# One list replaced: a hand-over of the emission order of a fused SSM convolution and SwiGLU kernel

## The chip, the cores and the metric

The kernel runs on one core of a Trainium2 chip. The metric is the time of one execution on the device in microseconds (us). The engines are called as in the profile: PE (TensorE's matmuls) and PEld (its weight loads), DVE (VectorE), ACT (ScalarE), POOL (GpSimd) and SP (SyncE, which here only issues transfers).

## The reference

Everything is bf16 with S = 2048 rows, D = 640 columns and F = 1728 hidden columns. The first half is a gated long convolution, the second a SwiGLU layer, both with a residual:

```python
k_shift = sum(k_pad[:, t:t + S] * shift_k[:, 3 - t] for t in range(4))   # 4 taps down the rows
kv = k_shift * v
y = irfft(rfft(kv, 2 * S) * rfft(ssm_k, 2 * S))[:S]      # causal convolution, one filter of S taps a column
h = x + layernorm(x) * (y + kv * ssm_D)                  # x is A_q
n = layernorm(h)
out = h + (silu(n @ w_gate) * (n @ w_up)) @ w_down
```

## The kernel before

**Tiling.** The 2048 rows are cut into 4 blocks of 512. A block's columns of numbers are turned into a spectrum by matmuls with a constant basis WF (512 x 512, loaded once) and back by WI. `X0` to `X3` are the spectra of the blocks of kv, `G0` to `G3` those of the blocks of the filter ssm_k. Block j of the convolution needs X0 G_j + X1 G_(j-1) + ... + X_j G_0, which DVE multiplies and adds up (`mac`, L707 and L746/L747). Then come `inverse` (L813: matmuls with WI at L878, DVE's L892 that gates with the normalised row and adds the residual, giving h), the second layernorm (`norm` L760 on POOL for a few small numbers a row, `applied` L802 on DVE or ACT for the rows, L804/L807), `turn_h` (L911: h is transposed, by PE at L926 or by a DMA at L919) and `ffn` (L966). The FFN of block j (called f0 to f3) runs beside the convolution of block j + 1; f3 alone has nothing beside it.

**FFN.** The 1728 hidden columns are 13 chunks of 128 and one of 64. Two chunks at a time are computed for gate and up (`by_four` L1001; matmuls at L1022): ACT takes the silu of the gate's PSUM tile (L1014) and copies the up tile (L1012), DVE multiplies (L1016). Chunk 12 and the last 64 columns are done by `odd_by_four` (L1025). In f3 its steps have these numbers: 880 and 881 are the projections of chunk 12's gate and up into the two halves of one PSUM tile, 882 the silu of the first half (L1032), 883 the copy of the second half (L1033), 884 their product; 885 to 888 are the same for the last 64 columns (L1037 to L1039). The down projection (L1110) goes row tile by row tile through three cuts of the 14 chunks (in f3, row tile 0: 889 to 891, and so on). For the last row tile of f3 each cut is made in two parts, the first 384 columns and the last 256: 904, 906 and 908 are the three cuts of the first part, 905, 907 and 909 of the second. DVE adds the residual out of PSUM (910 for the first part, 912 for the second, both L1127) and SP sends each part out (911, 913, L1129). In the other blocks ACT copies the sum (L1116) and POOL issues a DMA that adds it to the output (L1117).

**The plan and its order.** Every step above is one of 914 numbered steps of a plan (`Plan`), each a small group of instructions of one engine or one transfer. `ORDER` (L71 to L107) is a list of all 914 numbers. The kernel emits the steps in that sequence, so each engine executes its own steps in the sequence of the list, and a DMA queue starts its transfers so. A negative entry -n stands for step n - 1 done on its other engine:

```python
            if n < 0:
                op.eng, op.ns, op.fn = op.other
                if op.rest:
                    op.rest.fn = None
```

The other engine of an ACT eviction (a copy out of PSUM; `evict` L256, `taken` L354) is DVE. That of a weight load on SP (`load` L264, `load_w` L932) is POOL's DMA queue. That of one of ACT's two shifted copies of k per block (`load_two` L546, `put` L561) is a DMA that POOL issues (L563). That of an `applied` step on ACT is DVE. A product of k and v may read PSUM straight on DVE, in place of ACT's copy and DVE's multiply (L658 in place of L664 and L665).

The list also sets the buffers: there are 12 large SBUF buffers (`big`, used for inputs, spectra, weights and h), 5 row buffers (`row`) and 4 PSUM tiles of two banks (`ps`), and `Plan.schedule` (L189) gives each step that opens a buffer the one that has been free longest by the order of the list. Waits between engines follow from the buffers and data, not from the list's numbers.

**Queues.** SP issues the input loads, the constants, the transposing transfers of k and h, most weights and the last output rows, one behind the other; a load whose buffer is still in use holds up those behind it. POOL computes the norms' small numbers and the diagonal fills `pairs` (steps 17 to 21, L1185, each four tensors of 128 x 64) for the convolution of k by taps, and issues the adding DMAs and the weights and copies moved to it.

**Start.** The first loads are k0, g0, x0, v0 and WF (step 28), then by the list 366 (the last gate and up columns of f0), 205 (x1) and 30 (the negated basis, `minus`). PE turns k0 (L610), turns g0 (L471), does the taps of k0 (L639), and begins X0 at 13.21 us.

Of the kernel before, what the change touches and what calls it, by code (L numbers as in the profile page):

```python
# [68 lines left out]
TW = PAD + BLK  # L69
CUTS = ("X0", "G0", "m", "i")  # L70
ORDER = [  # L71
# [36 lines left out]
SLOTS = {'S': 8, 'big': 12, 'kT': 0, 'tT': 1, 'row': 5, 'sg': 0, 'co': 2, 'ps': 4, 'sm': 6}  # L108
HOME = {t: "big" for t in ("scr", "x", "ld", "t4", "hT", "wgu", "diag")} | {"o": "row", "ps_c": "ps", "ps_f": "ps"}
SPLIT = ((0,), (1,))  # L110
# [1220 lines left out]
```

## Time and profile before

Three executions of the kernel before gave a median of 262.64 us, 262.58 to 263.24. The profiled execution took 262.15 us.

| | |
|---|---|
| profiled execution: its own time | 262.15 us |
| its span, first to last instruction | 260.3 us |
| what lies around the span | 1.85 us |
| mean granted TensorE clock | 0.996 |
| PE busy | 251.7 us, 97% |
| DVE busy | 199.8 us, 77% |
| ACT busy | 180.3 us, 69% |
| POOL busy | 102.3 us, 39% |
| X0 begins (first L375) | 13.21 us |
| f0's projections begin (first L1022) | about 50.7 us |
| last matmul ends | 256.37 us |

Stages are read off PE's timeline: 0 to 13.2 is loading, k0 and g0; 13.2 to 50.7 the spectra X0, G0, G1 and X1, the taps of k1 and block 0 up to its transposed h; from there to 238 FFN projections and down projections lie between the matmuls of the later blocks' convolutions, and from 211 on f3 is alone; 238 to 256.4 is the last chunk and the down projection of f3, and the rest the last add and transfer. In the profile a PE group counts as busy from its first to its last matmul, so a wait of some tens of ns between matmuls shows as a lower pace and not as idle time. The idle time ahead of a group stands in brackets with what ended it.

### The profile page before, as it was taken

The numbers are of one execution on the slowest core, as the hardware profiler recorded it, in microseconds if no ns is written. First come the engines' busy times: TensorE is split into PE (matmuls) and PEld (weight loads), VectorE is DVE, ScalarE is ACT, GpSimd is POOL, SyncE is SP. The second block draws the span as 40 slices with busy tenths as digits, with TensorE's granted clock in tenths as the row PEclk, the third lists the DMA queues.
The fourth block names the chain that finished last, engine by engine and source line by source line (L and its number), as shares of the span: only waits on it lengthen the run. The fifth ranks groups of instructions, "written<-read, shape, count | busy, mean of one in ns | idle before, by whom it ended". The sixth has DMA issues, their size and how long they took to land.

```text
span 260.3 us, 4687 instructions
## 1 busy us (share of the span) xinstructions
PE 251.7 (97%) x1802; PEld 154.4 (59%) x1818; DVE 199.8 (77%) x262; ACT 180.3 (69%) x296; POOL 102.3 (39%) x114
## 2 busy tenths in 40 slices
PE   8999899999999999999999999999999999998993
PEld 7967567654655577754564577544457754443672
DVE  4589999999999999999999999999998100013113
ACT  3798999989999897797887987354595034446000
POOL 7952740007817983613029943129950041000000
PEclk9999999999999999999999999999999999999998
DMA  6996999979999999798958867769394575000002
GB/s 222 389 255 127 274 269 345 187 191 290 297 227 195 238 213 131 166 189 210 220 105 158 231 168 167 152 148 221 71 280 102 113 186 81 0 0 0 3 25 76
DMA packets 64335, 45.05 MB, mean 173 GB/s; under 512 B 30997, under 2 KB 59930, under 8 KB 64314
## 3 DMA queue, kind: packets, MB, share of 16 engines
q1 hardware_dynamic: 58576, 32.96, 51.0%
q0 software_dynamic: 5728, 11.80, 23.4%
q8 instruction: 14, 0.23, 0.4%
q14 instruction: 7, 0.06, 0.1%
q10 hardware_dynamic: 10, 0.01, 0.0%
HBM read 30.01 MB, written 4.59 MB: 133 GB/s over the span
## 4 chain that ended last, share of the span: by engine, by line
PE 84%; ACT 6%; DMA 4%; DVE 3%; issue 1%; SPq 1%; DVEq 0%; ACTq 0%
PE ps L1022 44%; PE ps L1110 23%; PE ps L375 10%; PE ps L878 4%; DMA WF<-const_wf 4%; PE ps L648 2%; ACT S L364 2%; ACT big L364 1%; DVE row L892 1%; ACT big L473 1%; DVE big L905 0%; ACT co L1012 0%; PE ps L471 0%; DVE big L658 0%; ACT big L928 0%
## 5 line engine op out<-in xcount | busy, mean ns | idle before, releaser
L1022 PE MATMUL ps<-big,big 128*128 128x512 bf16 x524 | 119.3, 379 | 1.8 <-ACT co L1033 1.0
L1022 PEld LDWEIGHTS <-big 128*128 128x128 bf16 x540 | 52.5, 98 | 61.3 <-issue 1.3
L1110 PE MATMUL ps<-wd,tT 128*128 128x320 bf16 (+2 forms) x416 | 60.6, 299 | 0.0
L1110 PEld LDWEIGHTS <-tT 128*128 128x128 bf16 x416 | 40.7, 98 | 16.3
L1016 DVE TENSOR_TENSOR tT<-tT,co 128x2048 bf16<-128x2048 bf16 x12 | 14.6, 1219 | 34.3 <-ACT tT L1014 28.7
L375 PE MATMUL ps<-big,WF 128*128 128x320 bf16 x240 | 39.1, 298 | 1.3 <-ACT big L364 1.0
L1014 ACT ACTIVATE tT<-ps 128x1024 bf16<-128x1024 f32 x24 | 24.4, 1025 | 19.8 <-PE ps L1022 19.7
L747 DVE TENSOR_TENSOR S<-S,big 128x2560 bf16<-128x2560 bf16 x23 | 34.3, 1492 | 0.8
L746 DVE TENSOR_TENSOR big<-S,S 128x2560 bf16<-128x2560 bf16 x23 | 34.1, 1484 | 0.2
L1012 ACT CAST co<-ps 128x1024 bf16<-128x1024 f32 x24 | 24.1, 1010 | 10.4 <-PE ps L1022 10.1
L375 PEld LDWEIGHTS <-WF 128*128 128x128 bf16 x240 | 23.1, 97 | 13.0 <-issue 2.0
L757 ACT ACTIVATE row<-big 128x640 bf16<-128x640 bf16 x32 | 23.7, 741 | 3.4 <-DVE big L905 1.4
L1117 POOL DMA_DIRECT2D out_dram<-row x12 | 12.2, 1211 | 26.9 <-ACT row L1116 26.9
L807 ACT ACTIVATE row<-big,sm 128x640 bf16<-128x640 bf16 x21 | 19.0, 927 | 1.6 <-POOL sm L789 1.2
L364 ACT CAST S<-ps 128x640 bf16<-128x640 f32 (+1 forms) x35 | 19.0, 590 | 1.5 <-PE ps L375 1.5
L364 ACT ACTIVATE big<-ps 128x640 bf16<-128x640 f32 (+1 forms) x23 | 15.3, 714 | 2.2 <-PE ps L375 2.2
L1116 ACT CAST row<-ps 128x640 bf16<-128x640 f32 x12 | 8.0, 697 | 11.9 <-PE ps L1110 11.2
L278 POOL DMA_DIRECT2D big<-row x8 | 7.0, 929 | 21.5 <-DVE row L892 21.1
L1185 POOL TENSOR_SCALAR pairs<-row,taps 128x64 bf16<-128x64 bf16 x20 | 13.9, 718 | 0.1
L775 POOL TENSOR_TENSOR sm<-sm 128x4 f32<-128x4 f32 x6 | 12.4, 2070 | 2.8 <-ACT row L796 2.6
L892 DVE SCALAR_TENSOR_TENSOR row<-row,ps 128x640 bf16<-128x640 bf16 x16 | 12.7, 814 | 0.8 <-PE ps L878 0.7
L278 POOL DMA_DIRECT2D S<-big x2 | 2.6, 1288 | 26.6 <-ACT co L1012 19.6
(110 smaller groups left out, 339.6 us busy)
## 6 DMA issues: line engine op xcount, KB each, us to landing
big<-in_B_w_gate_dram SPq DMA_DIRECT2D x17, 320.0 KB, 5.8
big<-in_B_w_up_dram SPq DMA_DIRECT2D x15, 320.0 KB, 5.1
big<-in_B_w_up_dram POOLq DMA_DIRECT2D x9, 320.0 KB, 6.6
big<-in_A_ssm_k_dram SPq DMA_DIRECT2D x4, 640.0 KB, 6.7
big<-in_A_q_dram SPq DMA_DIRECT2D x4, 640.0 KB, 7.2
big<-in_A_v_dram SPq DMA_DIRECT2D x4, 640.0 KB, 5.8
big<-in_B_w_gate_dram POOLq DMA_DIRECT2D x7, 320.0 KB, 5.1
wd<-in_B_w_down_dram SPq DMA_DIRECT2D x1, 2080.0 KB
```

Of the source, the lines that this page charges most:

```text
L364: (lambda: nc.scalar.activation(dst(), src(), ACT.Copy, scale=2.0)) if twice else (lambda: nc.scalar.copy(dst(), src())),
L375: nc.tensor.matmul(ap(ps)[:, h, 0:NH], w, ap(src)[:, r, h * NH:(h + 1) * NH], start=(first and i == 0), stop=(last and i == len(rs) - 1), ...
L746: nc.vector.tensor_mul(flat2(b), X.part(xs), H.part(hs))
L747: f(A.part(dst), A.part(dst), flat2(b))
L757: act(825, lambda r=r, junk=junk: nc.scalar.activation(ap(junk), ap(x)[:, r, :], ACT.Square, scale=D ** -0.5, accum_out=sm(s, 1)[:, r:r + ...
L807: nc.scalar.activation(ap(row), ap(x)[:, r, :], ACT.Identity, bias=sm(s, 5)[:, r:r + 1], scale=sm(s, 4)[:, r:r + 1])
L892: nc.vector.scalar_tensor_tensor(two(ap(t)), two(ap(t)), 1.0, half(ap(ps)), op0=ALU.mult, op1=ALU.mult, accum_out=sm(s, 0)[:, r:r + 1])
L1012: act(1010, lambda ps=ps: nc.scalar.copy(ap(co)[:, at:at + 2, :], ap(ps)), src, [(co, gi % 2)])
L1014: act(1010, lambda ps=ps: nc.scalar.activation(ap(tT)[:, c:c + 2, :], ap(ps), ACT.Silu), src, [done(range(c, c + 2), ROWS)])
L1016: dve(1220, lambda: nc.vector.tensor_mul(ap(tT)[:, c - 2:c + 2, :], ap(tT)[:, c - 2:c + 2, :], ap(co)), [co], [done(range(c - 2, c + 2), R ...
L1022: nc.tensor.matmul(ap(ps)[:, i, :], ap(w)[:, k, off:off + P], ap(hT)[:, k, :], start=(k == 0), stop=(k == KT - 1))
L1110: nc.tensor.matmul(ap(ps)[:, hf, to:to + n], t, ap(wd)[:, c, col + (hf - hs[0]) * NH:col + (hf - hs[0]) * NH + n], start=(c == order[0]), ...
```

## The change

Only the list `ORDER` is replaced. Its first and last lines before and after:

```diff
 ORDER = [
-    23, 4, 0, 1, 2, 5, 7, 6, 22, 31, 3, 39, 40, 8, 29, 13, 26, 27, 14, 15, 37, 38, 10, 24, 12, 9, 28, 11, 42, 33, 35, 41, 36, 57,
-    366, 55, -35, 43, 137, -57, 133, 205, 30, 192, -59, 134, 59, -61, 49, 50, 46, 132, -45, 51, 130, 52, -48, 136, 200, 45, -54,
...
-    846, 855, 865, 841, 857, 864, 866, 872, 873, 849, 858, 876, 885, 886, 874, 875, 824, 819, 881, 883, 887, 880, 894, 895, 882,
-    884, 899, 889, 904, 905, 888, 900, 896, 897, 901, 890, 891, 906, 908, 907, 909, 898, 892, 902, 893, 903, 910, 911, 912, 913]
+    0, 2, 31, 1, 4, 5, 7, 10, 6, 8, 16, 13, 12, 11, 22, 29, 26, 37, 27, 14, 3, 15, 23, 28, 42, -39, 9, 35, -37, 24, 39, 205, 40,
+    33, 41, 34, 55, 57, -57, -59, 137, 59, 134, 49, 30, -61, 132, 43, -45, 50, 51, 19, 63, 46, 366, 45, 52, 64, 68, 136, -48, 130,
...
+    872, 873, 829, 845, 846, 836, 837, 858, 874, 864, 885, 886, 865, 880, 881, 841, 866, 882, 883, 887, 875, 899, 900, 884, 888,
+    901, 902, 903, 894, 889, 904, 895, 906, 890, 896, 908, 910, 911, 891, 897, 905, 892, 898, 893, 907, 909, 912, 913, 824]
```

The steps and what each computes stay the same; PE does the same matmuls in another sequence from its fourth step on. The steps that change engine or queue:

| steps | before | after |
|---|---|---|
| evictions of k0: 34 | DVE | ACT |
| evictions of k0: 36, 38 | ACT | DVE |
| evictions of X0: 69, 75, 86, 88 | DVE | ACT |
| evictions of X0: 77, 96 | ACT | DVE |
| `applied` of block 2: 515, 519 | DVE | ACT |
| `applied` of block 2: 517 | ACT | DVE |
| `applied` of block 3: 736 | DVE | ACT |
| one product of k3 and v3: 656 | ACT's copy and DVE's multiply | DVE straight out of PSUM |
| shifted copy of k3: 614 | SP's queue | POOL's queue |
| shifted copy of k3: 615 | ACT, an instruction | POOL's queue, a DMA |
| weights of f1: 525, 541, 549, 559, 566 | SP's queue | POOL's queue |
| weights of f1: 533 | POOL's queue | SP's queue |
| weights of f2: 775 | SP's queue | POOL's queue |
| weights of f2: 742, 758, 766 | POOL's queue | SP's queue |
| weights of f3: 833 | SP's queue | POOL's queue |
| weights of f3: 825, 826, 842, 868 | POOL's queue | SP's queue |

Places in the sequence that the rest of the text speaks of:

- SP at the start: 28 (WF), then 205, 30, 366 (before 366, 205, 30). Later g2's load 398 comes ahead of 32 (WI), and 204 (v1) ahead of 339 and 340 (weights of f0).
- DVE at the start: 63 (an eviction of g0's transposes) comes ahead of 53 (the last product of k0 and v0).
- POOL at the start: the fills of `pairs` 19, 21, 17, 18 and 20 all come ahead of the shifted copies of k1, 202 and 203 (before, 19 came behind them).
- ACT around 45 us: 274 (part of the first norm of block 1) and 248 (an eviction of X1) come behind block 0's steps.
- f0 begins with 344 (before with 345, ahead of which came 425, matmuls of the spectrum G2).
- Norm of block 3: ACT's 697 comes behind 745, and POOL's 704 follows it; 570 (a silu of f1) is read by the first cuts of f1's down projection, of which 603 is one.
- The end of f3: 885, 880, 881, 882, 883, 887 (before 885, 881, 883, 887, 880, 882); 908, 910, 911 ahead of 905, 907, 909, 912, 913 (before all matmuls ahead of 910).

64 rows, old and new, of the table ORDER are left out of this document.

## The prediction

> **What bounds the kernel now.** I read the head of the page first, then the chain of work that ended last, then busy time by stage (columns: PE, PEld, DVE, ACT, POOL, PE clock, DMA share, GB/s), then PE's timeline around every gap, and the timeline of the end.
>
> ```profile
> span 260.3 us, 4687 instructions
> PE 251.7 (97%) x1802; PEld 154.4 (59%) x1818; DVE 199.8 (77%) x262; ACT 180.3 (69%) x296; POOL 102.3 (39%) x114
> ...
> PE 84%; ACT 6%; DMA 4%; DVE 3%; issue 1%; SPq 1%; DVEq 0%; ACTq 0%
> ```
>
> TensorE is busy 97% of the span and holds 84% of the chain, so the order can gain only what PE loses: idle time, and stretches where its matmuls wait for one another's buffers and are still counted busy.
>
> ```profile
> 13.20:23.50 10.30, 10.26 (x76) 6.99 (x77) 9.37 (x20) 9.54 (x27) 4.67 (x11) 1.00 0.99 207
> 23.50:50.00 26.50, 24.71 (x259) 18.03 (x258) 26.02 (x51) 26.12 (x51) 8.05 (x7) 1.00 1.05 258
> 50.00:90.00 40.00, 39.73 (x272) 21.71 (x276) 39.74 (x39) 37.93 (x56) 21.28 (x17) 1.00 1.00 241
> ...
> 238.00:256.40 18.40, 17.39 (x122) 11.65 (x120) 4.36 (x6) 3.04 (x5) 0.00 (x0) 1.00 0.05 19
> 256.40:260.30 3.90, 0.00 (x0) 0.00 (x0) 0.89 (x2) 0.00 (x0) 0.00 (x0) 0.76 0.25 82
> ```
>
> Between 50 and 238 PE is full. Time is lost in 23.5 to 50 (1.79 us idle, with DVE and ACT full), in 238 to 256.4 (1.01) and after the last matmul (3.90). These lines of PE's timeline show the gaps:
>
> ```profile
> 29.52 1.89 PE L375 MATMUL ps<-big,WF 128*128 128x320 bf16 x12 [0.81 <-ACT big L364]
> 35.56 0.44 PE L471 MATMUL ps<-ident,big 128*128 128x128 bf16 x5 [0.46 <-DVE row L892]
> ...
> 239.91 1.24 PE L1022 MATMUL ps<-big,big 128*128 128x512 bf16 x5 [0.98 <-ACT co L1033]
> ```
>
> and these the end and ACT's one wait for POOL:
>
> ```profile
> 239.28 0.58 ACT L1033 CAST co<-ps 128x512 bf16<-128x512 f32 x1
> ...
> 256.10 0.27 PE L1110 MATMUL ps<-wd,tail 128*128 128x256 bf16 x1
> 256.40 0.89 DVE L1127 TENSOR_TENSOR row<-ps,big 128x384 bf16<-128x384 f32 x2 [0.89 <-PE ps L1110]
> ```
> ```profile
> 29.16 6.32 POOL L1185 TENSOR_SCALAR pairs<-row,taps 128x64 bf16<-128x64 bf16 x4
> 35.52 0.92 ACT L807 ACTIVATE row<-big,sm 128x640 bf16<-128x640 bf16 x1 [0.37 <-POOL pairs L1185]
> ```
>
> **The change, part by part.** The matmuls are the same, so their time cancels.
>
> *The start, 0 to 13.2.* x1's load (205, 640 KB) now follows WF (28) directly, with minus (30) and the tail gate/up weights (366) behind. PE's first X0 matmul waits for WF, issued at 2.91 and landed at 13.17; PE had run dry 0.28 us before. WF's packets share the queue either way; I take 0, bounds -0.28 (PE is not ready earlier) to +1.0 (a tenth of its 10.3 us).
>
> On SP, g2's load (398, 640 KB) passes ahead of WI (32, 512 KB), which before landed at about 28 and is first used at 31.25; all packets of both were through by 30.4, so 0 with 0.85 us to spare.
>
> *X0 and G0, 13.2 to 23.5.* On DVE the g0 eviction 63 (0.49) is now ahead of the last kv0 product 53, which ends at 14.36 instead of 13.96; PE's transposes 61 behind it start 0.4 us later. Two X0 evictions less go to DVE (77, 96 instead of 69, 75, 86, 88; 0.49 each), so by 21.5 DVE stands 0.15 us ahead of before, and ACT takes two more (0.42 each). Sum 0, bounds -0.15 and +0.4.
>
> *Block 0 to the first FFN matmul, 23.5 to 50.7.* The last fill of `pairs` (19) went from behind the two T copies (29.16 to 35.49) to the start of POOL's order, so the row it held is free and the 0.37 us wait of ACT is gone. Two ACT steps that stood ahead of block 0's transposes (274, 0.82, and 248) now stand behind them. By my walk through ACT's and DVE's orders with these durations, the turned block is ready about 0.6 us earlier. The first FFN projection (344) then starts at about 49.9; before, 345 started at 50.69, but with 425 (0.54 us) done ahead of it that now comes later, so 50.15 is break-even: a gain of 0.27. DVE is full from 21.5 to 46 and caps it at about 0.6; the lower end is the first rival's.
>
> *50 to 238.* PE stands on its own work, so a late step costs nothing until its slack is gone. The tightest: silu 570 (f1) ahead of the cut 603 of its down projection at 148.4, 0.3 us; weights 541 of f1, now POOL's, issued after the output add 387 (about 113), landing at 118 to 119.7 for a need at 120.7; the norm of block 3 (704 on POOL, 7.75 us from 178.25 to 186.0 before) starts at about 180.4 because ACT's 697 now comes behind 745, so its `applied` rows start at 188.3 and the PSUM tiles behind them have 0.3 to 1 us. The third T copy of block 3 (615, 2.34 us of ACT at 126) becomes a POOL transfer with more than 10 us to spare, 614 with it. Queues: f1 has 6 weights on POOL's queue (2 before), f2 4 (6), f3 5 (8). Behind 541 on POOL stand 615, the output add 382, block 2's swap 489 and the weights 566 and 559, which find the same queue order as before but for the issue's 1.2 us; behind 704 the adds 592 and 607 and three weights of f3, read from 211 on, over 20 us later. Cover is the 5 to 10 us that each weight buffer is held ahead of use; a median 320 KB piece lands in 6.6 and 5.1 us from POOL, 5.8 and 5.1 from SP, so I take 0, with 0 to +1.6 as bounds (a further 2 us on the norm, as between 7.75 and the 8.7 us another norm took plus a queued DMA issue of 1.2, at 0.8 a us).
> The Trainium skill speaks against that move: "SBUF — State Buffer", section on who interferes with whom, says that descriptors of POOL's transfers are starved while VectorE is in its fast modes. The medians above do not show it for weights; T<-T does take 8.7 us from POOL against 3.8 from SP. If 541 took 8.7 too, it would land at 121.7, 1.0 us late.
>
> *The last chunk, 238 to 256.4.* 880 and 881 fill halves 0 and 1 of one PSUM tile. Before, 881 and ACT's copy of its half (883, L1033) came first and 880 waited for the copy's end: the 0.98 us at 239.91. Now both are emitted ahead of 882 and 883. The product 884 and the tail's 888 are ready 2.05 us after the last projection, and 901, which reads them, is 2.72 us behind it: no new wait. Gain 0.98.
> The skill's "PSUM — Partial Sum Buffer", section on bank collisions, has only engines in the same bank and quadrant of partitions collide, and these halves are two banks; by it the wait was the order's and not the chip's, and 0.98 goes.
>
> *The tail.* Before, the last two DVE adds (910 of 384 columns, 912 of 256) both ran behind the last matmul, 0.89 together, because 910 was emitted behind 909. Now 908 and 910 come ahead of 905, 907 and 909, so only 912 follows. Its share by columns is 0.36, by an even split 0.45; I take 0.42 (with a fixed part, as the planner has it), a gain of 0.47. The last transfer (913, 64 KB, landing 1.6 us after issue) is the last in both.
>
> Sum: 0.27 + 0.98 + 0.47 = 1.72. The profiled execution's own time is 262.15 (span 260.3 and 1.85 around it), so 260.43; the median of the runs is 0.49 above it, so 262.64 - 1.72 = 260.9.
>
> **The rivals.**
> 1. *Slower: the shifted copy of k1 meets v1's load.* v1 (204, packets of 5120 B) was issued at 32.53, behind 339 (packets of 512 B, 30 to 50 ns each); now it goes ahead of 339, at about 31.5, when the T copies on POOL's queue move (packets of 4112 B, 318 ns, 32 to 36.1). The copies have 10 packets on each DMA engine, v1 8 of 200 to 340 ns. PE's convolution of k1 (L648, 37.55) already waited 0.26 for the copy. If all 8 go between, the copy lands up to 8 x 0.34 = 2.7 us later. Behind it only 224 (0.54) can fill PE. Then 2.7 - 0.5 = 2.2 is lost, DVE's chain to block 0 loses as much of the 0.27, and 260.9 + 2.2 + 0.3 = 263.4; with minus' and x1's swap costing the +0.4 to +1.0 too, 263.8 to 264.4. It decides from a landing later than about 39.9. For it: DMA share is 1.05 in this stage; against: SP's next free buffer may come after the copies. "DMA: Bandwidth & Descriptors", section on queues and completion order, lets an engine alternate between queues packet by packet, which is what this rival needs; the trace's interleaved packets at 33 to 36 agree.
> 2. *No change: a new wait in the middle.* The norm of block 3 or f1's weights come 1 to 2 us beyond their slack: 0.8 to 1.6 back, 261.9 to 262.5.
> 3. *No change: the stall at 239.91 stays.* If 880 waited for the PSUM tile's former reader and not the copy, the gain is 0.74: 261.9 or, with 0.4 lost at 14, 262.3. Against it: 880 starts 0.05 us after the copy's end.
>
> **How the numbers follow.** Forecast 0.57 (260.9, own range 260.1 to 261.8: 0.33 better by DVE's cap, 0.28 by an earlier WF and 0.15 at 21.5; 0.9 worse by the +0.4 at 14 and 0.5 of the norm's price), rival 1 0.24, rival 2 0.14, rival 3 0.05. 0.3%, 0.79 us, is about what a measurement of this kernel can tell from no change: faster is below 261.85, slower above 263.43. Faster: the forecast, and a little of 2 and 3: 0.58. Slower: rival 1 from its decisive point up, with parts of 2 added to it: 0.24. Same: 0.18. The range runs from 260.1 to 263.9, leaving out the dearest sums of rival 1 and the best case.
>
> **What would show it.** Right: no gap on PE by ACT L1033 near 239; one DVE L1127 of about 0.4 behind the last matmul; ACT L807 without a wait for `pairs`; the first L1022 at about 49.9. Rival 1: PE's L648 waiting for DMA T<-T past 39.9. Rival 2: gaps on PE by `big` at 118 to 125 or by ACT L807 at 188 to 211. The prediction is wrong if PE's busy share between 13 and 50 falls, or if gaps appear between 50 and 238 where there are none now.

## The result and the profile after

The kernel after takes 261.16 us (median of 8 runs, 260.52 to 262.36), the kernel before 262.61 us (median of 8 runs, 261.96 to 263.24): a ratio of 0.9949, 95% interval 0.9935 to 0.9962. The forecast was 260.9 with 260.1 to 263.9 around it. The profiled execution of after took 261.3 us, 0.85 us less than the profiled one of before (262.15), where the medians differ by 1.45; the two profiles are thus 0.6 us closer to each other than the kernels are, so a difference of that size has to be looked for in more than one profile.

The head of the page of after:

```profile
span 259.6 us, 4700 instructions
PE 251.3 (97%) x1803; PEld 154.2 (59%) x1818; DVE 198.6 (77%) x259; ACT 180.0 (69%) x297; POOL 97.0 (37%) x115
...
PE 78%; ACT 9%; DMA 6%; DVE 2%; issue 2%; SPq 1%; ACTq 0%; DVEq 0%
```

The chain has 6% of DMA in it where before had 4%, which was WF alone. The busy time of after by stage, in the columns that the prediction named (start and end of the stage, its length, then PE, PEld, DVE, ACT, POOL, PE clock, DMA share, GB/s):

```profile
23.50:50.00 26.50, 24.71 (x260) 18.07 (x259) 26.05 (x50) 25.81 (x50) 2.71 (x4) 1.00 1.04 268
50.00:90.00 40.00, 38.90 (x266) 20.89 (x269) 38.70 (x38) 38.34 (x57) 15.60 (x13) 1.00 1.03 216
...
238.00:256.40 18.40, 18.05 (x126) 12.03 (x123) 5.23 (x8) 2.89 (x5) 0.00 (x0) 1.00 0.07 25
256.40:259.60 3.20, 0.00 (x0) 0.00 (x0) 0.11 (x1) 0.00 (x0) 0.00 (x0) 1.00 0.21 69
```

From 238 on PE no longer idles (its work simply ends at 256.05), but from 50 to 90 it is idle for 1.10 us where before had 0.27. PE's timeline has that gap, and the line of the first FFN projection:

```profile
49.70 1.24 PE L1022 MATMUL ps<-big,big 128*128 128x512 bf16 x4
...
81.11 1.25 PE L1022 MATMUL ps<-big,big 128*128 128x512 bf16 x4 [0.78 <-DMA big<-in_B_w_up_dram]
```

The end of after, from the timeline of all engines: one last add of 0.42 us, where before had two in 0.89.

```profile
255.78 0.27 PE L1110 MATMUL ps<-wd,tail 128*128 128x256 bf16 x1
256.09 0.42 DVE L1127 TENSOR_TENSOR row<-ps,big 128x256 bf16<-128x256 f32 x1 [0.59 <-PE ps L1110]
```

A measure of the end by itself is the stretch from f3's first projection to the end of the last matmul. PE's timeline from 203 on begins f3 with this line in before

```profile
210.72 28.22 PE L1022 MATMUL ps<-big,big 128*128 128x512 bf16 x127
```

and with this one in after:

```profile
211.53 29.30 PE L1022 MATMUL ps<-big,big 128*128 128x512 bf16 x132
```

Before needs 256.37 - 210.72 = 45.65 us from there, after 256.05 - 211.53 = 44.52: the end gains 1.13 us on PE, and 0.38 more behind it (the rest of the span is 3.93 us before and 3.55 after). But f3 begins 0.81 us later in this profile of after. The end gave all of the gain and the stages ahead of it took part of it back. The experiments take the three parts (start, middle, end) one by one.

Both signs by which the prediction would have called itself wrong are in this trace. PE's busy time from 13.2 to 50 fell from 34.96 us to 34.67, about by a gap of 0.30 us at 14.14 (a_53 below shows no cost of it). And a gap stands between 50 and 238 where before has none, the 0.78 us at 81.11; the middle does cost time.

### The profile page after: what moved, and what is told of

Its sections match the earlier page's. It is cut to its first block, busy times and chain, and to the rows that moved or that the text cites. A ratio compares the mean times of both kernels' runs of the same rounds, so it can differ in the third digit from the quotient of the medians.

```text
span 259.6 us, 4700 instructions
## 1 busy us (share of the span) xinstructions
PE 251.3 (97%) x1803; PEld 154.2 (59%) x1818; DVE 198.6 (77%) x259; ACT 180.0 (69%) x297; POOL 97.0 (37%) x115
## 4 chain that ended last, share of the span: by engine, by line
PE 78%; ACT 9%; DMA 6%; DVE 2%; issue 2%; SPq 1%; ACTq 0%; DVEq 0%
PE ps L1022 40%; PE ps L1110 23%; PE ps L375 10%; DMA big<-in_B_w_up_dram 4%; PE ps L878 3%; DMA big<-in_A_q_dram 3%; ACT T L565 2%; ACT big L364 1%; ACT S L364 1%; PE ps L648 1%; ACT row L757 1%; ACT big L664 1%; ACT big L473 1%; ACT tT L1014 1%; DVE row L892 1%
## 5 line engine op out<-in xcount | busy, mean ns | idle before, releaser
L1110 PE MATMUL ps<-wd,tT 128*128 128x320 bf16 (+1 forms) x416 | 60.3, 299 | 0.0
L807 ACT ACTIVATE row<-big,sm 128x640 bf16<-128x640 bf16 x23 | 20.3, 922 | 3.8 <-POOL sm L789 2.8
L364 ACT CAST S<-ps 128x320 bf16<-128x320 f32 (+1 forms) x36 | 19.4, 583 | 0.3
L1116 ACT CAST row<-ps 128x640 bf16<-128x640 f32 x12 | 8.1, 691 | 14.2 <-PE ps L1110 13.2
L719 DVE TENSOR_TENSOR big<-S,S 128x2560 bf16<-128x2560 bf16 (+1 forms) x10 | 12.2, 1218 | 0.1
L959 POOL DMA_DIRECT2D big<-in_B_w_gate_dram x8 | 9.1, 1137 | 8.1 <-PE ps L1022 7.8
```

Of the source, the lines that this page charges most:

```text
L364: (lambda: nc.scalar.activation(dst(), src(), ACT.Copy, scale=2.0)) if twice else (lambda: nc.scalar.copy(dst(), src())),
L807: nc.scalar.activation(ap(row), ap(x)[:, r, :], ACT.Identity, bias=sm(s, 5)[:, r:r + 1], scale=sm(s, 4)[:, r:r + 1])
L1110: nc.tensor.matmul(ap(ps)[:, hf, to:to + n], t, ap(wd)[:, c, col + (hf - hs[0]) * NH:col + (hf - hs[0]) * NH + n], start=(c == order[0]), ...
```

## The experiments

Ratios are to the kernel before on the same chip; "us" are medians.

**The swap of 880 alone.**

```diff
-  819, 881, 883, 887, 880, 894
+  819, 881, 880, 883, 887, 894
```

> The kernel before with one step moved: the projection 880 is emitted ahead of 883 and 887, directly behind 881. If the 0.98 us stall at 239.91 belongs to the order (880 queued behind ACT's copy of the other half of its PSUM tile), the gap on PE by ACT L1033 is gone and the time falls by about 1.0 us, ratio 0.996. If 880 waits for the former reader of the tile, the gap stays in part and the time falls by 0.25 us or less, ratio 0.999 to 1.000.

261.41 us, ratio 0.9965 (0.9947 to 0.9982), so 0.92 us. PE's timeline of b_swap, here from f3's first projection and from the last ones on, has no bracket between the projections and the down projection:

```profile
210.58 29.30 PE L1022 MATMUL ps<-big,big 128*128 128x512 bf16 x135
...
237.78 2.11 PE L1022 MATMUL ps<-big,big 128*128 128x512 bf16 x9
239.72 3.02 PE L1110 MATMUL ps<-wd,tT 128*128 128x320 bf16 x21
```

No wait of PE for ACT L1033 is left, and from f3's first projection (210.58) to the end of the last matmul (255.09) it is 44.51 us: 1.14 us less than before and as long as in after to 0.01 us. The stall was the order's: ACT's copy 883 now runs behind 880, from 239.92.

**The early add of the last row tile alone.**

```diff
-  908, 907, 909, 898, 892, 902, 893, 903, 910, 911, 912, 913]
+  908, 910, 911, 907, 909, 898, 892, 902, 893, 903, 912, 913]
```

> The kernel before with the last row tile's first add and transfer (910, 911) emitted directly behind 908, ahead of 907 and 909. Theory: only 912 follows the last matmul, DVE L1127 there takes 0.42 us in place of 0.89, and the time falls by about 0.47 us, ratio 0.998. Rival: the last transfer sets the end and 913 waits behind 911 either way, so nothing is gained, ratio 1.000.

262.82 us, ratio 1.0014 (0.9999 to 1.0029): nothing gained, and the 0.4 us lost is just short of being told from nothing. The rival's time came, but not by its cause, as the span behind the last matmul did get shorter (3.65 us, 3.93 before). The timeline of b_tail:

```profile
255.39 0.56 DVE L1127 TENSOR_TENSOR row<-ps,big 128x384 bf16<-128x384 f32 x1 [4.17 <-PE ps L1110]
...
256.00 1.03 PE L1110 MATMUL ps<-wd,tT 128*128 128x256 bf16 x8 [0.65 <-DVE row L1127]
```

The add does go ahead of 907 now, but PE's next matmuls write the other half of the same PSUM tile and wait 0.65 us for the add that reads the first half. It is the stall of 880 over again: in both, the wait is for the reader of the other half of the tile, and which of the two waits goes by the order of emission. Only one of the two adds is behind the last matmul, but that ends 0.81 us later, counted from f3's first projection (46.46 us against 45.65).

**The whole end of after on before.** All steps from 885 on in after's sequence, where the last cut of another row, 891, stands between 908 and 905 (819, 824, 841, 865, 866 and 875 go to after's places with them):

```diff
-  906, 908, 907, 909, 898, 892, 902, 893, 903, 910, 911, 912, 913]
+  908, 910, 911, 891, 897, 905, 892, 898, 893, 907, 909, 912, 913, 824]
```

> The order of before, with the steps from 885 on in the sequence that after has: the swap of 880 and the early 910 together, with the other rows' matmuls (891, 897, 905, 892) between 908 and 907. Theory: the swap gives 0.98 us, and the early add gives its 0.47 us here because those matmuls run while DVE reads the PSUM tile that 907 waits for; the time falls by 1.4 to 1.5 us, ratio 0.9945, and so all of after's net gain is its end. Rival: only the swap counts and the tail gives nothing, 0.9 to 1.0 us, ratio 0.9964.

260.63 us, ratio 0.9929 (0.9911 to 0.9947), so 1.86 us, more than the 1.4 to 1.5 that were expected. From f3's first projection (210.78) to the end of the last matmul (255.29) it is 44.51 us again, and the span ends 3.31 us later (3.91 in b_swap). So with 891 as a filler the early add does pay, 0.6 us in these profiles; the two ratios are 0.9 us apart, with intervals that touch. PE's timeline of b_end shows the filler, 891's eight matmuls in two lines, and DVE's add 910 (from 252.71, 0.56 us) ends while they run:

```profile
252.51 0.98 PE L1110 MATMUL ps<-wd,tT 128*128 128x320 bf16 x6
253.33 0.43 PE L1110 MATMUL ps<-wd,tail 128*128 128x320 bf16 x2
253.60 1.58 PE L1110 MATMUL ps<-wd,tT 128*128 128x256 bf16 x13
```

The third line is 905 and 907 with no wait ahead of it. b_end, the end of after on the rest of before, is 0.2% faster than after in the medians, but the two intervals overlap.

**The tail put back in after.**

```diff
-  908, 910, 911, 891, 897, 905, 892, 898, 893, 907, 909, 912
+  908, 891, 897, 905, 892, 898, 893, 907, 909, 910, 911, 912
```

> After, with 910 and 911 put back behind 909, so that DVE does both adds behind the last matmul. Theory: 0.89 us on DVE after the last matmul in place of 0.42, the time 0.4 to 0.5 us above after's, ratio to the kernel before 0.9965. Rival: the end is set by the last transfer and not by the adds, the time is after's, ratio 0.995.

261.61 us, ratio 0.9963 (0.9949 to 0.9977): 0.45 us above after in the medians. DVE's timeline has the two adds in one line again:

```profile
255.72 0.89 DVE L1127 TENSOR_TENSOR row<-ps,big 128x384 bf16<-128x384 f32 x2 [0.70 <-PE ps L1110]
```

The rest of the span behind the last matmul is 4.22 us (3.55 in after), 0.67 more. That agrees with the prediction's 0.47 in sign and about in size; by the times alone, whose intervals overlap, it would not be told from nothing.

**The start alone.** After's order up to the first FFN projection, then before's.

```diff
-  ORDER = [before]
+  ORDER = [after's entries up to 344 (without it), then before's that are left]
```

> The order of after up to the first step of the first FFN (344), then the remaining steps in the order of before. It holds the gain of the start alone. Theory, from the two traces: X0 begins at 12.80 in place of 13.21 and the first FFN projection about 0.35 us earlier by work done, and before's middle has no wait for weights, so the time falls by 0.3 to 0.4 us, ratio 0.9986; the gap of 0.98 near 239.5 and the 0.89 us tail are there. Rival: the start's gain is used up by 50, as work that was postponed comes later, and the time is the one before, ratio 1.000.

262.38 us, ratio 0.9994 (0.9978 to 1.0009): 0.16 us, not told from nothing. The profile speaks for the rival: f0's first projection comes at 50.54 (before 50.69, with the same work done), but PE then waits 0.18 us at 54.66 for a copy of ACT, and f3's first projection is at 210.90, no earlier than in the four kernels with before's start and middle (210.58 to 210.78).

**The start put back.** Before's order up to the first FFN projection, then after's.

```diff
-  ORDER = [after]
+  ORDER = [before's entries up to 345 (without it), then after's that are left]
```

> Before's order up to the first FFN projection, then after's middle and end. Theory: it lacks the start's 0.27 us of the prediction and keeps the late adding transfer of after's middle, so it is 0.1 to 0.4 us slower than after, ratio to the kernel before 0.996; ACT's wait of 0.37 us for pairs near 35.5 is there. Rival: the start is worth nothing, ratio 0.995.

261.40 us, ratio 0.9960 (0.9947 to 0.9973), 0.29 us behind after's ratio, with intervals that overlap. ACT's wait for `pairs` is back (0.39 us), and PE's convolution of k1 waits 0.31 us for its copy, as in other kernels with before's start (0.46 in b_v2). The second line is a gap that neither after nor before has, where the two parts are joined, so the 0.29 us is not the start's alone:

```profile
37.98 2.18 PE L648 MATMUL ps<-pairs,T 128*128 128x64 bf16 x60 [0.31 <-DMA T<-T]
...
52.91 0.70 PE L375 MATMUL ps<-big,WF 128*128 128x320 bf16 x4 [0.56 <-ACT big L364]
```

**63 behind 53 on DVE, in after.**

```diff
-  -45, 50, 51, 19, 63, 46, 366, 45, 52, ... -54, 65
+  -45, 50, 51, 19, 46, 366, 45, 52, ... -54, 63, 65
```

> After, with the eviction 63 behind the product 53 on DVE, as before has them. Theory of the prediction: the 0.30 us gap ahead of PE's transposes at 14.14 goes, but it was recovered by 21 to 24 us in any case, so the first FFN projection and the time stay within 0.15 us of after's, ratio 0.995. Rival: a delay of PE ahead of X0's evictions goes through to block 0, and the time falls by 0.3 us, ratio 0.994.

261.10 us, ratio 0.9944 (0.9927 to 0.9961), the same as after. The gap of 0.30 us at 14 is gone and the first FFN projection is at 49.89, where four kernels with that gap and after's start and middle have 49.60 to 49.89. In this profile X0 even began at 13.39, in a_348 at 12.66, and block 0 was ready at the same time (49.89 and 49.87). In these profiles what PE gains or loses ahead of 21 us is absorbed. (Later this one has a gap of 0.41 us at 109.39, for a copy of ACT, which none of the other profiles has.)

**368 earlier.** The load that PE waited for at 81.11 goes ahead of three loads of 640 KB.

```diff
-  365, 327, ...  408, 270, ... 608, ... 348, ... 368
+  365, 368, 327, ... 408, 270, ... 608, ... 348
```

> After, with the 80 KB load 368 (the last part of f0's last weights) issued directly behind 365, ahead of the 640 KB loads 408 and 608. In the profile of after the projection 374 stands still for 0.78 us at 81.11 for this load, whose packets came from 78.0 to 80.2. Theory: the gap goes, nothing takes its place, and the time falls by 0.7 to 0.9 us against after (ratio to the kernel before about 0.9915). Rival: another weight or the transposes behind it are late by as much, or the gap is not in most runs of after, and the time is after's, ratio 0.995.

260.56 us, ratio 0.9939 (0.9912 to 0.9966), with runs in two groups (259.96 to 260.56 four times, 261.45 to 261.85 three times). PE has no gap from 50 to 90 in its profile, which is that of its fastest run, but the theory's 0.7 us off after is not shown by an interval that holds after's ratio, and the upper group says that something else still comes late in some runs.

**348 ahead of 608, in after.**

```diff
-  408, 270, ... 356, ... 608, ... 349, ... 348
+  408, 270, ... 356, ... 348, 608, ... 349
```

> After, with the weights 348 ahead of the 640 KB load 608 on SP, as before has them. If 368 is late because everything on SP behind 608 waits for 608's buffer until 69.47, then 348 is through before that, 368 lands about 1 us earlier, the 0.78 us gap at 81 shrinks to 0.2 us or less, and the time falls by 0.5 to 0.8 us against after (ratio 0.992). If 368 is late because the DMA engines share their time with POOL's 640 KB transfer from 73 to 78, then the order ahead of it changes little: the gap stays over 0.5 us, ratio 0.995.

260.73 us, ratio 0.9934 (0.9917 to 0.9951): 0.4 us below after, not told from nothing, as the interval holds after's ratio. The gap at 81 is gone; in the profiled run, the slowest of its six at 261.57, there is a larger one at another place, for weights that come in behind the x2 load on SP (issued at 63.95, landing 9.7 us later, beside 270):

```profile
73.74 1.25 PE L1022 MATMUL ps<-big,big 128*128 128x512 bf16 x5 [1.10 <-DMA big<-in_B_w_gate_dram]
```

So the 0.78 us at 81 seems to be one face of a lateness that shows now here, now there. Three of the six profiles of after's middle (after, a_tail0, a_53, a_368, a_348, b_start) have a gap between 60 and 90, and just these three have DVE waiting at 69 to 70 for 270, the transfer on POOL's queue that adds DVE's product into a sum in SBUF. DVE's timeline in after, a_348 and a_tail0:

```profile
69.43 1.49 DVE L747 TENSOR_TENSOR S<-S,big 128x2560 bf16<-128x2560 bf16 x1 [0.47 <-DMA S<-big]
```
```profile
70.02 1.49 DVE L747 TENSOR_TENSOR S<-S,big 128x2560 bf16<-128x2560 bf16 x1 [0.87 <-DMA S<-big]
```
```profile
70.39 1.49 DVE L747 TENSOR_TENSOR S<-S,big 128x2560 bf16<-128x2560 bf16 x1 [1.53 <-DMA S<-big]
```

The landing of 270 also opens a buffer on SP: in after and a_tail0 the load 608 is issued directly behind it, at 69.47 and 70.4, and all of SP's queue follows 608; in a_348 it is the weights 348 that wait for 270. Behind DVE comes the inverse transform of block 1 (in a_tail0 PE waits 0.64 us at 78.62 for DVE's sum). In the six profiles of after's middle 270 lands 8.3 to 10.9 us after its issue, and the three over 9.5 are those with the waits (9.9 in after, 10.3 in a_348, 10.9 in a_tail0); in six profiles of before's middle it takes 7.0 to 8.7, and neither DVE waits for it nor has PE a gap between 60 and 90. In before it lands at 67.8 and is read at 69.38, 1.6 us later; after would read it at 68.96 and has it at 69.4. The DMA view shows the median of 270 and the one other transfer of its kind. Lines of the DMA view of before, and of after:

```profile
S<-big POOLq DMA_DIRECT2D x2, 640.0 KB, 7.4
```
```profile
S<-big POOLq DMA_DIRECT2D x2, 640.0 KB, 8.3
```

Packet by packet: in before 270's pieces of 2560 B are alone on the DMA engines and move at 82 a us from 63 to 65. In after v2's load (407, issued at 58.16) and the weights 357 (60.16), which stand behind one another on SP on either side of 270's issue at 59.46, are still moving; 270 starts in earnest 1 us later and moves at 62 to 74 a us beside pieces of 512 and 5120 B.

**The same loads back to before's places, in after.** 365 ahead of 404, 407 directly behind it.

```diff
-  404, ... 315, ... 365, ... 314, ... 407, ... 357, 408
+  365, ... 404, 407, 315, ... 314, ... 357, 408
```

> After, with two loads on SP put back where before has them: 365 (160 KB of f0's last weights) ahead of 404, and 407 (v2, 640 KB) directly behind 404. In the profiles of after's order the adding transfer 270 (S<-big, 640 KB on POOL's queue, issued at 59.5) shares the DMA engines with 407 and 357 and lands near 69; DVE then waits for S<-big by 0.5 to 1.5 us (L747 near 69 to 70) and one of three late followers stops PE between 73 and 82 for 0.6 to 1.1 us. Theory: with the loads out of its way 270 lands by 67.5, the wait of DVE for S<-big and PE's gap go, and the time is 0.5 to 0.9 us below after's, ratio to the kernel before 0.992. Rival: the gaps come from the longer list of POOL's weights or from another place, and the ratio stays at 0.995.

261.72 us, ratio 0.9977 (0.9966 to 0.9988): slower than after, a miss. The transfer itself did what the theory says: it runs alone at 82 pieces a us, lands 7.0 us after its issue and DVE waits for S<-big no more. But it is issued 2.2 us later (61.65 in place of 59.46), since the move changed who gets which buffer:

```profile
58.19 1.49 DVE L741 TENSOR_TENSOR big<-S,S 128x2560 bf16<-128x2560 bf16 x1 [1.91 <-PE ps L375]
```

DVE's product, which the transfer adds, now opens a buffer that PE is still reading. PE's gaps (0.54 us at 74.26 and 0.65 at 79.41) are both for DVE, which has had no other wait since, so they fit this one; no run takes it away alone.

**The reverse, in b_end.** 365 between 315 and 314, then 407 and 357 ahead of 408.

```diff
-  404, ... 407, 315, ... 314, ... 408, 270, ... 356, 357
+  404, ... 315, ... 365, 314, 407, ... 357, 408, 270, ... 356
```

> The order of b_end (before with after's end) with after's sequence of these loads on SP: 365 between 315 and 314, then 407 and 357 ahead of 408. Theory: 270 lands near 69 here too, DVE waits for S<-big and PE has a gap of 0.5 to 1 us between 70 and 82, so the time is 0.5 to 0.9 us above b_end's, ratio to the kernel before 0.996. Rival: before's middle has room for it, no gap, and the ratio stays at 0.993.

262.52 us, ratio 1.0009 (0.9997 to 1.0022): 1.9 us lost against b_end, over twice what was expected. The transfer is spread out as foreseen (43 to 66 pieces a us from 65 to 74, landing 11.0 us after its issue), but DVE does not wait for it; DVE waits 2.87 us for a buffer that PE reads, and PE's three gaps between 76 and 81 (0.28 to 0.62 us) are for DVE:

```profile
65.45 1.49 DVE L746 TENSOR_TENSOR big<-S,S 128x2560 bf16<-128x2560 bf16 x1 [2.87 <-PE ps L1022]
```

So these two runs show that the places of three loads on SP decide 0.7 to 2 us, by the queue and by the buffers together. How much of after's loss is the one and how much the other they don't separate, and no run here moved the queue without the buffers. That the late landing of 270 is the cause of the lost time is thus argued from the profiles and not shown.

**Both ends of after without its middle.** After's order to the first FFN projection, before's from there, after's from 885 on.

```diff
-  ORDER = [after]
+  ORDER = [after's entries up to 344 (without it), before's that are left, and after's from 885 on]
```

> After's order up to the first FFN projection, then before's, then after's end from 885 on: both ends of after without its middle. Theory: the start gives what a_start showed, 0.0 to 0.3 us, on top of b_end: ratio to the kernel before 0.992 to 0.993, the fastest so far or level with b_end. Rival: the start's order costs time when followed by before's middle, ratio 0.994 or more.

260.31 us (260.24 to 260.71, five runs), ratio 0.9922 (0.9911 to 0.9934): faster than both kernels, and as narrow in its runs as before is. Its interval ends just below where after's begins. Against b_end it is 0.2 us faster, which is not told from nothing. From after it differs in the middle alone, and that is 0.0027 of 262.6, 0.7 us.

## Why the prediction was right, point by point

The total was met in part by luck: the end gave 0.3 to 0.4 us more than was forecast for it (1.76 in the profile of b_end, 1.86 by its ratio, for 0.98 + 0.47), the start about what was forecast at best, and the middle, taken at 0, took 0.7 back.

- **The last chunk: right, a little small.** 0.98 was forecast by the idle time; b_swap shows 1.14 us on PE's stretch and 0.92 by the ratio. The 0.16 between 0.98 and 1.14 fits the overlap that groups of matmuls have in the record where nothing stops them (in b_swap the projections from 237.78 end at 239.89 and the next group begins at 239.72) and that a stall takes away. By "PSUM — Partial Sum Buffer" of the Trainium skill, section on bank collisions, two engines in different banks don't collide, so the wait was not the chip's. b_swap and b_tail agree that it was the order's, as the wait went and came with the order of emission while the halves stayed where they are; no run here has PE write one half of a tile while another engine reads the other half.
- **The tail: the size right, the condition missed.** 0.47 was forecast; a_tail0 shows 0.45 in the medians and 0.67 in the profile, b_end against b_swap 0.6 in the profiles and 0.9 by the ratios. The step counted the add that goes and not the wait that it puts ahead of 907 and 909: what covers the add's 0.56 us is the 1.1 us of 891 in the new list, and without it (b_tail) the gain is gone and 0.4 us with it. The step should have named that cover.
- **The start: not shown.** 0.27 was forecast; the ratios give 0.16 (a_start), 0.18 (c_mix against b_end) and 0.29 (after against b_start, with the gap at its join), none told from 0. By profiles, f0's first projection is at 50.56 to 51.21 in six kernels with before's start, which less the 0.54 us of 425 is 50.29 on average, and at 49.60 to 49.89 in six with after's start and middle, on average 49.80. That is 0.5 us, but 0.3 without the two profiles with before's start in which the copy of k1 was late (b_start and b_v2); and with before's middle behind it nothing of it is left at f3 (a_start). The smaller steps came as described: the 0.4 us late transposes showed as a 0.30 us gap and were recovered (a_53). ACT's wait for `pairs` is gone.
- **50 to 238: the term that was mis-sized.** It was taken as 0, with 0 to 1.6 as bounds; after against c_mix shows 0.7 us. It was not lost at the tight places that were named: 541 was issued at 113.90 and its projection began at about 121.2 without a gap, the norm of block 3 (704) ran from 181.07 to 188.17 as forecast within 0.7 us, and no profile shows a gap there. In the profiles with a gap it was lost between 60 and 82, where the step said that weights have 5 to 10 us of cover. The cover was read from median landing times, and the adding transfer 270, which is no weight but stands in the same queues, was not costed at all: in before it landed 1.6 us ahead of its reader, and the 0.27 us of PE's idle time from 50 to 90 did not tell how little.
- **The starvation rule.** By "SBUF — State Buffer" of the Trainium skill, section on who interferes with whom, as the prediction reads it, 541 would have been late. It landed 5.6 us after its issue, at 119.5. But this case doesn't try the rule: the same section says that a `tensor_tensor` has no 2-port mode, and from 112 to 121 DVE ran nothing else. POOL's 320 KB weights take 7.2 and 6.7 us in the medians against 5.1 and 6.6 before, so they are slower or no faster, but the cover holds them.
- **Rival 1 fell.** v1 was issued at 31.50, as reckoned, ahead of 339, but its packets (5120 B) moved from 35 on, behind the T copies' (31 to 35.4), and L648 began at 37.06 with no wait for the copy. With before's start it waits up to 0.46 us.
- **Rival 2 happened in kind, a little below its lower price of 0.8,** at another place: 0.7 us, between 60 and 82 in the profiles that show a gap, and for neither f1's weights nor the norm.
- **Rival 3 fell** with b_swap.

The sum that the runs give is 1.8 to 1.9 for the end and 0 to 0.3 for the start, less 0.7 for the middle: 1.1 to 1.5 us, where the ratio says 1.34 and the medians 1.45.

## What to carry to other kernels

In this kernel a stall of PE behind a copy of the other half of its own PSUM tile is a matter of emission order: emit both writers ahead of the first reader, and have other matmuls ready where a reader must come early. When a list of steps is replaced, add up the transfers that add or copy inside the chip too, by their own slack, and look at what shares the DMA engines with them and at which step opens which buffer, because one moved load changes both. And when a long order is better at its ends and worse in its middle, cut it: the parts of two orders can be joined where the steps done agree. Look at the join as well, as it can have a gap of its own (0.56 us in b_start).

## What the runs showed of the hardware

- An adding transfer of 640 KB in pieces of 2560 B runs at 82 pieces a us when alone (before, 63 to 65; a_v2, 65 to 67), 62 to 74 beside pieces that are mostly of 512 B (after, 64 to 67), and 43 to 50 beside a mix of 512 and 5120 B (b_v2, 65 to 69). In b_v2 the 16 DMA engines together took the two queues' pieces about one for one: 50 against 52 in the us from 66, when 27 of the 52 had 5120 B, and 66 against 65 in the us from 72, when 5 had. So here the larger the other queue's pieces were, the slower the transfer went. The Trainium skill's "DMA: Bandwidth & Descriptors", section on queues and completion order, has an engine take turns between queues packet by packet; the counts agree with turns, but can't show how many pieces a turn has.
- Most kernels with after's middle spread in time: 260.24 to 262.63 us in a_53 and 260.52 to 262.36 in after, where 27 of the 30 runs of before in the first set of experiments lie within 0.8 us (261.94 to 262.68) and the five of c_mix within 0.5 (but the 23 of before beside a_53 span 1.5). That would fit a transfer which lands at the edge of its slack, late in three of six profiles of this middle, but it is not shown: the five runs of b_start, with the same middle, lie within 0.3 us (261.23 to 261.50).
- X0's first matmul began anywhere from 12.66 to 13.39 us in the fourteen profiles, and the first FFN projection did not follow it (49.87 in a_348, 49.89 in a_53, the earliest and the latest).
